# A planned attention and feed-forward kernel: weight buffers cut from two areas, and four output tiles by seven block products with sums made by adding transfers

## The chip, the cores and the metric
The kernel runs on one core of a Trainium2 chip. A time is what one execution takes on the device, in microseconds (us); the metric is the median of several executions. Engines are called by their short names: PE multiplies matrices, DVE and ACT do element-wise work, POOL is the fifth engine, SP issues transfers.

## The reference
Attention with a soft cap (batch 2, 12 heads, 448 positions, head size 64), and behind it two feed-forward layers over 896 tokens, 768 wide inside and out and 2048 in the middle:

```
x   = attention(q, k, v)                      # 896 x 768
g1  = s * relu(x @ w1_in)**2 + b              # 896 x 2048
y   = g1 @ w1_out                             # 896 x 768
h   = y @ w2_in
out = (h * clip(h + 3, 0, 6) / 6) @ w2_out
```
All in float32. The weights arrive as raw 64-bit numbers and are turned into float32 on the core.

## The kernel before
**Products.** Each operand is split in two float32r parts, hi (the rounded value) and lo (the rest). One product of a 128x128 weight block with 128x448 columns is three matmuls into one PSUM bank: lo weight with hi value, hi with lo, hi with hi (`matmuls`, L232). Tokens come in two halves of 448 (`bi` 0 and 1).

**w_in by seven products.** `strassen` (L673) takes two weight tiles and both token halves as 2x2 blocks, and computes the four results by seven block products instead of eight (Strassen's scheme in Winograd's form). The sums of weight blocks S1 to S4 are made on DVE (L575 to L578), the sums of the right-hand blocks T1 to T4 once for a layer on DVE by `minus`. p1 and p2 make one result; p6 and p7 are added onto a copy of p1 in a bank `bb`, with the sums d1 and d2 between them on DVE.

**w_out plainly.** Each layer's w_out has six 128-row tiles (`mt`), and its 16 blocks of the middle dimension come in two halves of 8. For each tile and token half, 8 products are added into a bank. The sum of the first half waits in a slot as `partial` and is copied back into a bank by ACT before the second half (L771). At layer 1's end ACT scales the bank by 1/6 (L791), and SP stores it.

**Weights.** `convert` fetches a raw tile (three buffers), ACT rescales it (L215), DVE shifts and merges bits (L223, L229); for w_in ACT makes the low bits first (L219). `parts` then makes hi on ACT (L543) and lo on DVE (L545). All of this works in one tile `w` of eight blocks; hi and lo lie in groups `gA` (two) and `gB` (two). Activations, sums and stores use 84 slots of 448 columns.

**Order.** `Plan` sets the order of the whole feed-forward part before anything is issued. Each task has an engine, a cost and tasks that it comes after; due times run backwards from PE's list, and a greedy pass hands each engine the most urgent task whose inputs and buffers are free (PE may choose among 36). The engines then run their queues in exactly that order: an instruction that waits holds up all behind it on its engine. What comes before, attention (to 91 us), is written out by hand.

Of the kernel before, what the change touches and what calls it, by code (L numbers as in the profile page):

```python
# [26 lines left out]
HF = KF // 2  # L27
# [7 lines left out]
BYTES = (True, False)  # L35
SLOTS_A, SLOTS_B = 36, 48
GROUPS = {"gA": 2, "gB": 2}
# [3 lines left out]
class Res:  # L41


    def __init__(self, kind, tile=None):
        self.kind, self.tile, self.left, self.held, self.order = kind, tile, 0, tile is not None, None


class Task:
    def __init__(self, engine, cost, run, after, use, number):
        self.engine, self.cost, self.run, self.use, self.number = engine, cost, run, use, number  # L50
        self.after = list(dict.fromkeys(t for t in after if t is not None))
        self.then, self.due, self.start, self.end = [], 1e9, None, None


class Plan:
# [5 lines left out]
    def __init__(self, sizes):  # L61
        self.tasks, self.sizes, self.pe = [], sizes, []
# [11 lines left out]
    def order(self):  # L74
# [3 lines left out]
        for t in reversed(self.tasks):  # L78
            for s in t.then:
                t.due = min(t.due, s.due - t.cost - self.LAG)  # L80
        for t in self.tasks:
            if t.soon is not None:
                t.due = min(t.due, max([a.due + a.cost for a in t.after if a.engine == "PE"], default=0.0) + t.soon)
        for t in reversed(self.tasks):
            if t.engine != "PE":
                for s in t.then:
                    t.due = min(t.due, s.due - t.cost - self.LAG)
        free = dict(self.sizes)
        banks, seen = 0, {}
# [12 lines left out]
        waiting = {e: [] for e in ("PE", "DVE", "ACT", "DMA")}  # L102
# [3 lines left out]
        for e in ("DVE", "ACT", "DMA"):  # L106
# [4 lines left out]

        def kind_of(u):
            kinds = u.kind if isinstance(u.kind, tuple) else (u.kind,)
            return next((k for k in kinds if free.get(k, 0) > 0), None)

        while left:
            moved = True
            while moved:
                moved = False
                for e, queue in waiting.items():  # L120
                    if idle[e] > now + 1e-9:
                        continue
                    for t in queue[:self.WINDOW] if e == "PE" else queue:
                        if any(a.end is None or a.end + (0 if a.engine == e else self.LAG) > now + 1e-9 for a in t.after):
# [4 lines left out]
                        for u in want:  # L129
                            k = kind_of(u)  # L130
                            if k is None or (u.kind == "bank" and u.order != next_bank):
                                ok = False
                                break
                            need[u] = k
                            free[k] -= 1
                        if not ok:
                            for k in need.values():
                                free[k] += 1
                            continue
                        for u, k in need.items():  # L140
                            u.held, u.kind = True, k
                            if k == "bank":
                                next_bank += 1
                        t.start, t.end = now, now + t.cost
                        idle[e] = t.end
# [5 lines left out]
            times = [x for x in idle.values() if x > now + 1e-9]  # L151
            times += [t.end + self.LAG for t in done[-80:] + ends if t.end + self.LAG > now + 1e-9]
# [4 lines left out]
            for t in [t for t in ends if t.end <= now + 1e-9]:  # L157
                ends.remove(t)
                done.append(t)
                for u in t.use:  # L160
                    u.left -= 1
                    if u.left == 0:
# [12 lines left out]
def attention_moe_moe(ctx: ExitStack, tc: tile.TileContext, qk, v, cap, w1i, w1o, s, b, w2i, w2o, out):  # L175
    nc = tc.nc
    const = ctx.enter_context(tc.tile_pool(name="const", bufs=1))
    sa = ctx.enter_context(tc.tile_pool(name="sa", bufs=SLOTS_A))
# [9 lines left out]
    whole = const.tile([128, 8, BL], F32, name="w")  # L188
    zeros = sa.tile([128, S], F32, name="zeros", tag="s")
    slot = lambda name, dt=F32R: sa.tile([128, S], dt, name=name, tag="s")  # L190
    x = [[[slot(f"x{p}{bi}{k}") for p in ("h", "l")] for k in range(KD)] for bi in range(B)]
    flat = whole.rearrange("p n m -> p (n m)")

    pools_w = {"gA": wp}
# [3 lines left out]

    def group(kind):
        n = 4 * BL if kind == "gA" else 3 * BL  # L200
        return [pools_w[kind].tile([128, n], F32R, name=f"{kind}{p}", tag=f"{kind}{p}", bufs=GROUPS[kind]) for p in ("h", "l")]
# [7 lines left out]
    def rescale(raw, n, bits, dve=False):  # L209
        up = raw_up(raw, n).bitcast(F32)  # L210
        up = up.rearrange("p (n m) -> p n m", m=BL) if len(bits.shape) == 3 else up
# [13 lines left out]
    def merge(raw, n, bits, mask=0x80000007, low=False):  # L225
        part = raw[:, :n, 0 if low else 1]
        part = part.rearrange("p (n m) -> p n m", m=BL) if len(bits.shape) == 3 else part
# [155 lines left out]
    def take(p):  # L383

        xu[p] = slot("xf", F32)
        nc.vector.tensor_copy(xu[p], pav.pop(p)[:, :S])

    def scale_x(p, engine=nc.vector.tensor_copy):
        bi, hp = divmod(p, H // 2)
        last = p >= P - 2  # L390
        if last:
            xu[p] = slot("xf", F32)
# [11 lines left out]
    first_groups, raws = {}, {}  # L404
# [4 lines left out]
    def early_region(i):  # L409

        if i < FIRST:
            return flat[:, i * CI:(i + 1) * CI]
        at = {FIRST: 1, FIRST + 1: 0, FIRST + 2: 4}[i]
        return whole[:, at:min(at + 4, 8):2, :] if at % 4 == 0 else whole[:, at:at + 3:2, :]
# [11 lines left out]
    def early_upper(i, dve=False):  # L426
        if i % 2 == 0:
            first_groups[i // 2] = group("gA")
        hi = first_groups[i // 2][0][:, i % 2 * CI:(i % 2 + 1) * CI]
        (nc.vector.tensor_copy if dve else nc.scalar.copy)(hi, early_region(i))  # L430

    def early_lower(i):
        hi, lo = (t[:, i % 2 * CI:(i % 2 + 1) * CI] for t in first_groups[i // 2])
        nc.vector.tensor_sub(lo, early_region(i), hi.bitcast(F32))

    def early_w(i, k):
        sl = slice(i % 2 * CI + k * 128, i % 2 * CI + (k + 1) * 128)
        return [t[:, sl] for t in first_groups[i // 2]]
# [11 lines left out]
    def feed_forward(sb):  # L450
# [529 lines left out]
```

## Time and profile before

| | us |
|---|---|
| three executions | 544.96, 540.43, 544.74 |
| their median | 544.74 |
| profiled execution, its own time | 539.42 |
| its span, first to last instruction | 537.6 |
| PE busy in the span | 529.6 |

The profile is of one execution. A matmul's shown length (366 ns for 448 columns) overlaps the next one's, so the distance from one start to the next is what a matmul costs PE. DVE and ACT instructions overlap a little too. In a chain of waits a row gives where a piece starts, how long it lasts and what it is.

### The profile page before, as it was taken

How to read it: one execution, taken by the hardware profiler on the slowest of the kernel's cores; microseconds unless marked ns; L12 is line 12 of the kernel's file. 1: busy time of each engine (PE TensorE's matmuls, PEld its weight loads, DVE VectorE, ACT ScalarE, POOL GpSimd, SP SyncE). 2: the span in 40 equal slices, each digit the busy share in tenths (PEclk: the TensorE clock that was granted, in tenths of full speed). 3: DMA queues.
4: the chain of work that ended last, by engine and by line, in shares of the span. 5: the costliest groups of instructions: out<-in, count | busy, mean ns of one | idle time of the engine just before them, and what ended most of it. 6: DMA issues, size and time to landing. Idle time of an engine off the chain costs nothing.

```text
span 537.6 us, 7211 instructions
## 1 busy us (share of the span) xinstructions
PE 529.6 (99%) x2768; PEld 437.4 (81%) x2768; DVE 412.6 (77%) x627; ACT 382.2 (71%) x521; POOL 0.6 (0%) x8
## 2 busy tenths in 40 slices
PE   8999999999999999999999999999999999999997
PEld 3232335998999999989999999999999999999996
DVE  2789999999997647889887888898756378997300
ACT  6999998696965657998567777964467479866201
POOL 0000000000000000000000000000000000000000
PEclk9999999999999999999999999999999999999999
DMA  8835412313036523224354233234544132236211
GB/s 316 334 111 185 129 36 87 122 36 95 30 97 214 176 81 117 99 79 133 102 177 152 89 112 99 78 95 113 176 173 144 66 98 79 79 116 187 77 51 51
DMA packets 17796, 64.36 MB, mean 120 GB/s; under 512 B 2402, under 2 KB 5730, under 8 KB 17634
## 3 DMA queue, kind: packets, MB, share of 16 engines
q1 hardware_dynamic: 17616, 63.75, 35.9%
q8 instruction: 21, 0.34, 0.3%
q10 hardware_dynamic: 146, 0.16, 0.1%
q14 instruction: 13, 0.11, 0.1%
HBM read 61.11 MB, written 2.79 MB: 119 GB/s over the span
## 4 chain that ended last, share of the span: by engine, by line
PE 92%; ACT 5%; DVE 2%; issue 1%; DVEq 0%; ACTq 0%
PE pf L234 39%; PE pav L234 30%; PE pz L234 10%; PE ps L267 5%; PE pav L293 4%; ACT t L275 2%; PE pav L290 1%; PE pz L330 1%; PE ps L271 1%; ACT raw L219 1%; ACT t L280 1%; PE pz L858 1%; ACT w L215 0%; DVE sl L488 0%; DVE gAl L545 0%
## 5 line engine op out<-in xcount | busy, mean ns | idle before, releaser
L229 DVE SCALAR_TENSOR_TENSOR w<-raw,w 128x512 uint32<-128x512 uint32 (+1 forms) x131 | 96.2, 758 | 21.8 <-ACT raw L219 20.5
L234 PE MATMUL pf<-sl,gBh 128*128 128x448 f32 x316 | 90.0, 366 | 0.0
L234 PE MATMUL pf<-sl,gAh 128*128 128x448 f32 x288 | 81.9, 366 | 0.0
L215 ACT ACTIVATE w<-raw 128x512 f32<-128x512 f32 (+1 forms) x79 | 58.4, 762 | 23.0 <-DMA raw<-in_w2o 9.0
L234 PE MATMUL pav<-sl,gAh 128*128 128x448 f32 x252 | 71.8, 366 | 0.0
L234 PE MATMUL pav<-sl,gBh 128*128 128x448 f32 x234 | 66.6, 366 | 0.0
L234 PEld LDWEIGHTS pf<-sl,gBh 128*128 128x128 f32 x316 | 59.4, 188 | 5.1
L234 PE MATMUL pf<-sl,gBl 128*128 128x448 f32 x158 | 57.9, 366 | 0.0
L234 PEld LDWEIGHTS pf<-sl,gAh 128*128 128x128 f32 x288 | 54.1, 188 | 4.4
L219 ACT ACTIVATE raw<-raw 128x768 uint16<-128x768 uint16 x29 | 55.7, 1966 | 0.1
L234 PE MATMUL pf<-sl,gAl 128*128 128x448 f32 x144 | 52.7, 366 | 0.0
L543 ACT CAST gBh<-w 128x1152 fp32r<-128x1152 f32 (+1 forms) x27 | 29.8, 1104 | 31.6 <-DVE w L229 14.0
L234 PEld LDWEIGHTS pav<-sl,gAh 128*128 128x128 f32 x252 | 47.3, 188 | 4.0
L223 DVE TENSOR_SCALAR w<-w 128x512 uint32<-128x512 uint32 (+1 forms) x80 | 37.4, 475 | 17.0 <-ACT w L215 16.7
L545 DVE TENSOR_TENSOR gBl<-w,gBh 128x1152 fp32r<-128x1152 f32 (+1 forms) x27 | 34.8, 1289 | 18.9 <-ACT gBh L543 18.9
L234 PEld LDWEIGHTS pav<-sl,gBh 128*128 128x128 f32 x234 | 43.9, 188 | 3.6
L234 PE MATMUL pav<-sl,gAl 128*128 128x448 f32 x126 | 46.1, 366 | 0.0
L545 DVE TENSOR_TENSOR gAl<-w,gAh 128x1536 fp32r<-128x1536 f32 (+2 forms) x26 | 38.9, 1496 | 9.4 <-ACT gAh L543 9.3
L543 ACT CAST gAh<-w 128x1536 fp32r<-128x1536 f32 (+2 forms) x26 | 33.1, 1274 | 16.6 <-DVE w L229 13.2
L234 PE MATMUL pav<-sl,gBl 128*128 128x448 f32 x117 | 42.8, 365 | 0.0
L280 ACT ACTIVATE t<-t 128x896 f32<-128x896 f32 x42 | 39.9, 950 | 1.2
L275 ACT ACTIVATE t<-ps 128x896 f32<-128x896 f32 x42 | 37.9, 902 | 3.3 <-PE ps L267 3.3
(161 smaller groups left out, 901.4 us busy)
## 6 DMA issues: line engine op xcount, KB each, us to landing
raw<-in_w1i SPq DMA_DIRECT2D x16, 768.0 KB, 5.5
raw<-in_w1o SPq DMA_DIRECT2D x24, 512.0 KB, 3.7
raw<-in_w2i SPq DMA_DIRECT2D x16, 768.0 KB, 4.9
raw<-in_w2o SPq DMA_DIRECT2D x24, 512.0 KB, 4.2
rqk<-in_qk SPq DMA_DIRECT2D x11, 448.0 KB, 4.4
out<-sl SPq DMA_DIRECT2D x12, 224.0 KB, 1.9
rb<-rows SPq DMA_DIRECT2D x10, 224.0 KB, 3.6
va<-in_v SPq DMA_DIRECT2D x1, 1344.0 KB, 14.0
```

The source lines that it names most:

```text
L215: nc.scalar.activation(bits, up, AF.Copy, scale=2.0**-112)
L219: nc.scalar.activation(by[:, :, 2], by[:, :, 1], AF.Copy, scale=2.0**-13, bias=0.5**14 - 0.5)
L223: nc.vector.tensor_scalar(bits, bits, 3, None, op0=ALU.logical_shift_left)
L229: nc.vector.scalar_tensor_tensor(out=bits, in0=part, scalar=29 if low else mask, in1=bits, op0=ALU.logical_shift_right if low else ALU.bit ...
L234: nc.tensor.matmul(ps[:, :S], w[a], rhs[r], start=start and i == 0, stop=stop and i == 2, skip_group_check=True)
L267: nc.tensor.matmul(ps[:, j, :S], raw_qk[p][rows, 1, c * 128:(c + 1) * 128], raw_qk[p][rows, 0, :], start=True, stop=True)
L271: nc.tensor.matmul(ps[keys, col, :S], raw_qk[p + o][rows, 1, NC * 128:], raw_qk[p + o][rows, 0, :], start=True, stop=True)
L275: nc.scalar.activation(u_t[n], u_ps.pop(n)[:, :, :S], AF.Tanh, scale=icap_r)
L280: nc.scalar.activation(u_t[n], u_t[n], AF.Exp, scale=cap_r)
L293: nc.tensor.matmul(pav[p][(top, end)[j], :S], va[bi][:, d, (2 * (p % 2) + j) * NC + c, :], u_t[n][:, j, :], start=(p % 2 == 0 and c == 0), ...
L543: nc.scalar.copy(part(0), cols)
L545: c = add("DVE", dve(n), lambda: nc.vector.tensor_sub(part(1), cols, part(0).bitcast(F32)), [a], [g])
```

## The change
Buffers of the feed-forward part are no longer slots and groups: two areas of SBUF are handed out in columns by the plan itself (`Space`), 448-column tiles from one end and weight tiles from the other. A weight tile's lo part is now written over the converted weight itself (`low_of`). So a tile of converted weights is held per pair, not one for all, and the plan can convert several pairs ahead. The sums S1 to S4 are made inside the pair's own tiles.

At layer 1's end the last four w_out tiles (`OUT_ORDER[2:]`) of the second half go by seven products, two tiles at a time: 28 products of three matmuls a pair instead of 32. For this the sums of g are needed, for each of four block pairs `j`: four chained sums over 448-column tiles. They are made by 16 transfers that add onto their destination, issued by POOL (`accumulate`), after ACT has negated two operands; ACT and DVE then split each sum into hi and lo (`split_sum`). `partial` is no longer copied into a bank for these tiles but added when the result leaves it, mostly on DVE. `LOWS` says for which of a pair's four raw tiles ACT makes the low bits. The planner also counts an arrival time behind transfers (`late`) and lets ACT start at most 30 us ahead of a due time (`AHEAD`).

```diff
-BYTES = (True, False)
-SLOTS_A, SLOTS_B = 36, 48
-GROUPS = {"gA": 2, "gB": 2}
+LOAD = 0.004, 3.0
+AHEAD = {"ACT": 30.0}
+SUM_ISSUE, SUM_LATE = 1.2, 6.0
+SEVENS = 2
+LOWS = (True, False, True, False)
+SPACE = 36 * S + 12 * CI, 48 * S + 6 * CI
...
+    def take(self, n):
+        for area in ((1, 0) if n == S else (0, 1)):
+            for a, b in self.free[area] if n == S else reversed(self.free[area]):
+                if b - a >= n:
+                    at = a if n == S else b - n
+                    self.cut(area, at, n)
+                    return area, at
+        return None
...
+        def parts(f, after, before=()):
+
+            h = res(f.n)
+            a = add("ACT", acts(f.n), lambda: nc.scalar.copy(t_of(h, F32R), f.tile), after, [f, h])
+            c = add("DVE", dve(f.n), lambda: nc.vector.tensor_sub(low_of(f), f.tile, h.tile.bitcast(F32)), [a, *before], [f, h])
+            return (h, f), [a, c]
...
+        def out_pair(layer, mts, half):
+
+            f1, f2, f3 = res(3 * CO), res(2 * CO), res(2 * CO)
...
+            s1 = sums(f1, 2, f2, 1, f3, 0, CO, nc.vector.tensor_add, [m21, m22])
+            s2 = sums(f2, 0, f1, 2, f1, 0, CO, nc.vector.tensor_sub, [m11, s1])
+            s3 = sums(f2, 1, f1, 0, f2, 1, CO, nc.vector.tensor_sub, [m11, s1])
+            s4 = sums(f3, 1, f1, 1, f2, 0, CO, nc.vector.tensor_sub, [m12, s2])
+            (g1, t1), (g2, t2), (g3, t3) = parts(f1, [m12, s1], [s2, s3, s4]), parts(f2, [s2, s3], [s4]), parts(f3, [s4])
...
+        def accumulate(r, other, after):
+
+            t = add("POOL", SUM_ISSUE, lambda: nc.gpsimd.dma_start(out=r.tile, in_=other.tile, accum_op=ALU.add), after, [r, other])
+            t.late = SUM_LATE
+            return t
...
+        def sums_of_g(half):
+
+            n = HF // 2
+            ops = {x: [] for x in ("T1", "T2", "T3", "T4")}
+            for j in range(n):
+                f = half * HF + j
+                (b11, e11), (b12, e12), (b21, e21), (b22, e22) = [GF[f + k, bi] for k in (0, n) for bi in range(B)]
+                n12, f12 = negative(b12, e12)
+                n21, f21 = negative(b21, e21)
+                d3 = accumulate(b22, n12, [f12, e22, *G[f + n, 1].tasks])
+                d1 = accumulate(n12, b11, [d3, e11])
+                d2 = accumulate(b11, b22, [d1, d3, *G[f, 0].tasks])
+                d4 = accumulate(n21, b11, [d2, f21])
+                for x, t, d, sign in (("T3", b22, d3, 1), ("T1", n12, d1, -1), ("T2", b11, d2, 1), ("T4", n21, d4, -1)):
+                    ops[x].append(split_sum(t, d, sign))
...
+                if m == 0:
+                    pe[mark:mark] = first
+                    pe.extend(fifth + sixth + second)
+                else:
+                    pe.extend(first + tail[:len(tail) // 3] + fifth + tail[len(tail) // 3:] + sixth + second)
+                tail = seventh + last
+            pe.extend(tail)
```

**How the order changes, place 1: DVE at the start of the feed-forward part.** PE's 181st matmul there needs the lo part of the second pair's first weight tile, a subtraction over 1536 columns. Names w, gAl are the old weight tiles and groups, sl slots; m and two numbers name a piece of the new areas. Before:

```order
L638 SCALAR_TENSOR_TENSOR sl_916<-sl_916,st_66 128x448
L229 SCALAR_TENSOR_TENSOR w_71<-raw_933,w_71 128x2x384
L576 TENSOR_TENSOR w_71<-w_71 128x384
L488 TENSOR_TENSOR sl_1118<-sl_1043,sl_1103 128x448
L488 TENSOR_TENSOR sl_1125<-sl_1049,sl_1105 128x448
L488 TENSOR_TENSOR sl_1134<-sl_1055,sl_1113 128x448
L577 TENSOR_TENSOR w_71<-w_71 128x384
L578 TENSOR_TENSOR w_71<-w_71 128x384
L488 TENSOR_TENSOR sl_1149<-sl_1065,sl_1120 128x448
L488 TENSOR_TENSOR sl_1154<-sl_1074,sl_1127 128x448
L545 TENSOR_TENSOR gAl_1143<-w_71,gAh_1142 128x1536
```

And now:

```order
L755 TENSOR_TENSOR m75_1042<-m35_106,m32_103 128x448
L290 SCALAR_TENSOR_TENSOR m70_1015<-raw_943,m70_1015 128x768
L599 TENSOR_TENSOR m70_1015<-m70_1015 128x384
L599 TENSOR_TENSOR m62_978<-m70_1015,m62_978 128x384
L599 TENSOR_TENSOR m62_978<-m70_1015 128x384
L553 TENSOR_TENSOR m81_1075<-m65_995,m74_1040 128x448
L553 TENSOR_TENSOR m82_1080<-m67_1002,m77_1053 128x448
L589 TENSOR_TENSOR m84_1087<-m70_1015,m80_1069 128x1536
L553 TENSOR_TENSOR m87_1103<-m73_1038,m78_1058 128x448
```

Counted from the first sum of x's blocks (98.96 us in the trace of before), 41 DVE instructions stood ahead of that subtraction, and 28 do now; most of the sums of x moved behind it.

**Place 2: PE and POOL at layer 1's end.** Before, PE ran 8 products of one tile and one token half after another; the last bank begins

```order
L234 MATMUL pav_912<-sl_3876,gBl_4397 128x448
L234 MATMUL pav_912<-sl_3893,gBh_4396 128x448
L234 MATMUL pav_912<-sl_3876,gBh_4396 128x448
L234 MATMUL pav_912<-sl_3853,gBl_4397 128x448
L234 MATMUL pav_912<-sl_3865,gBh_4396 128x448
L234 MATMUL pav_912<-sl_3853,gBh_4396 128x448
```

Now PE comes to the first operand that hangs on the last pair's g (T1 of j = 3, written m567_4487 and m569_4495), to T2 of j = 0 and to T1 of j = 2:

```order
L295 MATMUL pf_895<-m567_4487,m527_4275 128x448
L295 MATMUL pf_895<-m569_4495,m524_4251 128x448
L295 MATMUL pf_895<-m567_4487,m524_4251 128x448
L295 MATMUL pav_917<-m560_4456,m533_4306 128x448
L295 MATMUL pav_917<-m564_4470,m526_4273 128x448
L295 MATMUL pav_917<-m560_4456,m526_4273 128x448
L295 MATMUL pf_895<-m571_4505,m527_4275 128x448
L295 MATMUL pf_895<-m573_4515,m524_4251 128x448
L295 MATMUL pf_895<-m571_4505,m524_4251 128x448
```

Between the end of p7 of the last w_in pair (bank pf_915, whence g of block 15 comes) and the second of these rows stand 124 matmuls; up to the lo part of T2 of j = 3 stand 157, and of T4 of j = 3 211. POOL, which issued no transfer before, issues 16, of which these are the last 12 (destination first; j = 3 and j = 2 alternate with j = 1 and 0):

```order
L764 DMA m525_4267<-m491_4045 128x448
L764 DMA m529_4285<-m498_4078 128x448
L764 DMA m472_3941<-m509_4150 128x448
L764 DMA m458_3825<-m514_4184 128x448
L764 DMA m491_4045<-m496_4071 128x448
L764 DMA m498_4078<-m469_3917 128x448
L764 DMA m530_4291<-m472_3941 128x448
L764 DMA m528_4280<-m458_3825 128x448
L764 DMA m496_4071<-m525_4267 128x448
L764 DMA m469_3917<-m529_4285 128x448
L764 DMA m547_4386<-m496_4071 128x448
L764 DMA m544_4370<-m469_3917 128x448
```

m525_4267 takes d3 of j = 3, m491_4045 then d1, m496_4071 d2, m547_4386 d4: each waits until the one before it has landed.

**Place 3: DVE at layer 1's end.** Before, the last DVE rows were the conversion of the last two tiles:

```order
L545 TENSOR_TENSOR gAl_4342<-w_71,gAh_4341 128x1024
L223 TENSOR_SCALAR w_71<-w_71 128x512
L229 SCALAR_TENSOR_TENSOR w_71<-raw_4283,w_71 128x512
L223 TENSOR_SCALAR w_71<-w_71 128x512
L229 SCALAR_TENSOR_TENSOR w_71<-raw_4331,w_71 128x512
L229 SCALAR_TENSOR_TENSOR w_71<-raw_4283,w_71 128x512
L229 SCALAR_TENSOR_TENSOR w_71<-raw_4331,w_71 128x512
L545 TENSOR_TENSOR gBl_4397<-w_71,gBh_4396 128x1024
```

Now, from the sum d2 of the last w_in pair (it waits for p7) to the lo part of g's block 15, behind which POOL may issue d3 of j = 3:

```order
L728 TENSOR_TENSOR m523_4249<-pf_915,m506_4127 128x448
L599 TENSOR_TENSOR m507_4132<-m516_4195 128x512
L599 TENSOR_TENSOR m507_4132<-m516_4195,m507_4132 128x512
L599 TENSOR_TENSOR m504_4104<-m516_4195,m507_4132 128x512
L589 TENSOR_TENSOR m527_4275<-m516_4195,m524_4251 128x1536
L677 SCALAR_TENSOR_TENSOR m525_4267<-m525_4267,m523_4249 128x448
L677 SCALAR_TENSOR_TENSOR m529_4285<-m529_4285,pf_895 128x448
L285 TENSOR_SCALAR m522_4233<-m522_4233 128x512
L589 TENSOR_TENSOR m533_4306<-m507_4132,m526_4273 128x1024
L691 TENSOR_TENSOR m536_4318<-m525_4267,m531_4298 128x448
```

and some 25 rows further the lo parts that PE's rows above need (L773), behind weights of the second pair:

```order
L589 TENSOR_TENSOR m565_4476<-m537_4320,m558_4444 128x1536
L773 SCALAR_TENSOR_TENSOR m569_4495<-m491_4045,m567_4487 128x448
L589 TENSOR_TENSOR m570_4503<-m532_4304,m553_4417 128x1024
L773 SCALAR_TENSOR_TENSOR m573_4515<-m498_4078,m571_4505 128x448
```

Of the 37 DVE instructions from that d2 to the lo part of T1 of j = 3, 16 are over 448 columns, 13 over 512, two over 1536, two over 1024, and four are shifts over 512; before, nothing after the last block of g stood on DVE but conversions.

## Rows read from the trace of the kernel before

**Rows 1.** Page, part 1: busy time, share of the span, instructions.
```profile
PE 529.6 (99%) x2768; PEld 437.4 (81%) x2768; DVE 412.6 (77%) x627; ACT 382.2 (71%) x521; POOL 0.6 (0%) x8
```

**Rows 2.** Waits of PE: total us, times, longest us.
```profile
PE ps L267 <- ACT t L275: 1.0, 2, 0.7
PE pf L234 <- DVE gAl L545: 0.3, 1, 0.3
```

**Rows 3.** Chain of waits, feed-forward part: start us, us, what.
```profile
103.91 10.95 PE pav L234 x54
...
130.09 7.44 PE pf L234 x36
...
174.73 14.88 PE pav L234 x72
...
234.57 3.65 PE pf L234 x18
...
390.51 9.72 PE pf L234 x48
```

**Rows 4.** Timeline of PE at two starts: start us, us, what, idle before.
```profile
125.24 0.57 PE L234 MATMUL pf<-sl,gAh 128*128 128x448 f32 x2
126.11 0.47 PE L234 MATMUL pf<-xh,gAl 128*128 128x448 f32 x1 [0.30 <-DVE gAl L545]
...
229.96 0.57 PE L234 MATMUL pf<-sl,gBh 128*128 128x448 f32 x2
230.66 0.47 PE L234 MATMUL pz<-xh,gAl 128*128 128x448 f32 x1
```

**Rows 5.** Stretches: busy us of each engine, granted clock, DMA share.
```profile
460.00:480.00 20.00, 20.00 (x101) 18.53 (x100) 19.90 (x35) 14.48 (x27) 0.00 (x0) 1.00 0.34 107
480.00:500.00 20.00, 20.00 (x100) 18.54 (x99) 15.96 (x26) 12.36 (x21) 0.00 (x0) 1.00 0.56 177
500.00:520.00 20.00, 20.00 (x100) 18.53 (x99) 2.15 (x3) 3.77 (x6) 0.00 (x0) 1.00 0.13 47
520.00:540.00 20.00, 14.02 (x70) 12.64 (x68) 0.00 (x0) 1.64 (x4) 0.00 (x0) 0.93 0.12 46
```

**Rows 6.** Timeline of DVE, runs without a gap and the start.
```profile
98.96 1.69 DVE L717 TENSOR_TENSOR sl<-xf 128x448 f32<-128x448 f32 x3
...
124.30 1.75 DVE L545 TENSOR_TENSOR gAl<-w,gAh 128x1536 fp32r<-128x1536 f32 x1
...
471.67 2.75 DVE L654 TENSOR_TENSOR sl<-sl 128x448 fp32r<-128x448 f32 x5
...
492.29 1.90 DVE L229 SCALAR_TENSOR_TENSOR w<-raw,w 128x512 uint32<-128x512 uint32 x3
```

**Rows 7.** Groups by line and form, DVE: mean ns of one.
```profile
L654 DVE TENSOR_TENSOR sl<-sl 128x448 fp32r<-128x448 f32 x40 | 24.1, 619 | 2.5 <-ACT sl L648 2.1
L545 DVE TENSOR_TENSOR gAl<-w,gAh 128x1536 fp32r<-128x1536 f32 x14 | 24.5, 1753 | 2.6 <-ACT gAh L543 2.5
L545 DVE TENSOR_TENSOR gBl<-w,gBh 128x1024 fp32r<-128x1024 f32 x13 | 15.9, 1220 | 4.5 <-ACT gBh L543 4.5
L223 DVE TENSOR_SCALAR w<-w 128x512 uint32<-128x512 uint32 x48 | 19.8, 421 | 7.5 <-ACT w L215 7.4
```

**Rows 8.** Timeline of ACT: a run of casts, and the last instruction.
```profile
101.47 2.44 ACT L485 CAST sl<-sl 128x448 fp32r<-128x448 f32 x5
...
534.06 0.54 ACT L791 ACTIVATE sl<-pav 128x448 f32<-128x448 f32 x1 [4.33 <-PE pav L234]
```

**Rows 9.** DMA issues: KB each, median us to landing.
```profile
raw<-in_w2i SPq DMA_DIRECT2D x16, 768.0 KB, 4.9
out<-sl SPq DMA_DIRECT2D x12, 224.0 KB, 1.9
rb<-rows SPq DMA_DIRECT2D x10, 224.0 KB, 3.6
va<-in_v SPq DMA_DIRECT2D x1, 1344.0 KB, 14.0
```

More of the change, by code (lines that the diff above doesn't have):

```diff
@@ L51, in __init__ @@
         self.after = list(dict.fromkeys(t for t in after if t is not None))
-        self.then, self.due, self.start, self.end = [], 1e9, None, None
+        self.then, self.due, self.start, self.end, self.late = [], 1e9, None, None, 0.0
 class Plan:
@@ L79, in order @@
             for s in t.then:
[L80 removed]
+                t.due = min(t.due, s.due - t.cost - t.late - self.LAG)
+        made = {}
         for t in self.tasks:
+            made[t] = max([a.due + a.cost if a.engine == "PE" else made[a] for a in t.after], default=0.0)
             if t.soon is not None:
[L83 removed]
+                t.due = min(t.due, made[t] + t.soon)
         for t in reversed(self.tasks):
@@ L86, in order @@
                 for s in t.then:
-                    t.due = min(t.due, s.due - t.cost - self.LAG)
+                    t.due = min(t.due, s.due - t.cost - t.late - self.LAG)
         free = dict(self.sizes)
+        space = Space(SPACE, {(*u.at, u.n) for t in self.tasks for u in t.use if u.kind == "mem" and u.held} | set(self.taken))
         banks, seen = 0, {}
@@ L101, in order @@
                     free[u.kind] = free.get(u.kind, 0)
-        waiting = {e: [] for e in ("PE", "DVE", "ACT", "DMA")}
+        waiting = {e: [] for e in ("PE", "DVE", "ACT", "DMA", "POOL")}
         for t in self.tasks:
@@ L105, in order @@
         waiting["PE"] = list(self.pe)
-        for e in ("DVE", "ACT", "DMA"):
+        for e in ("DVE", "ACT", "DMA", "POOL"):
             waiting[e].sort(key=lambda t: (t.due, t.number))
@@ L123, in order @@
                     for t in queue[:self.WINDOW] if e == "PE" else queue:
-                        if any(a.end is None or a.end + (0 if a.engine == e else self.LAG) > now + 1e-9 for a in t.after):
+                        if e in AHEAD and now < t.due - AHEAD[e]:
+                            continue
+                        if any(a.end is None or a.end + (0 if a.engine == e and e != "POOL" else self.LAG) > now + 1e-9 for a in t.after):
                             continue
@@ L151, in order @@
             times = [x for x in idle.values() if x > now + 1e-9]
+            times += [t.due - AHEAD[e] for e in AHEAD for t in waiting[e] if t.due - AHEAD[e] > now + 1e-9]
             times += [t.end + self.LAG for t in done[-80:] + ends if t.end + self.LAG > now + 1e-9]
@@ new lines, in convert @@
+            a = None
+            if raw is None:
+                a = add("DMA", n * LOAD[0], lambda: load_raw(tile_of(), src, n), (), [r])
+                a.late = LOAD[1]
+            if stage < 1:
+                a = add("ACT", acts(n, True), lambda: rescale(r.tile, n, bits()), [a], [r, f])
+            l = add("ACT", 0.0022 * n, lambda: low_bits(r.tile, n), [a], [r]) if low and stage < 2 else None
+            a = add("DVE", dve2(n), lambda: shift(bits()), [a], [f])
+            if low:
+                return add("DVE", dve(n), lambda: merge(r.tile, n, bits()), [a, l], [r, f])
@@ new lines, in convert @@
+            a = add("DVE", dve(n), lambda: merge(r.tile, n, bits(), 0x80000000), [a], [r, f])
+            return add("DVE", dve(n), lambda: merge(r.tile, n, bits(), low=True), [a], [r, f])
+        def parts(f, after, before=()):
[3 more added lines that the diff above has]
+            return (h, f), [a, c]
```

373 lines of the change are left out of this document (210 added, 163 removed).

## The prediction
> **What bounds the kernel now.** I began with the busy shares, and the reader is to see there that PE works 99% of the span [rows 1]. Then the waits of PE: from the feed-forward part on there is one that the page counts, 0.3 us [rows 2]. The chain of waits shows that from 130 us on PE alone sets the end, matmul behind matmul. So what counts is the number of matmuls, the distance from one start to the next, and any wait that the change adds.
>
> The distance is not one number. In the chain it is 10.95/54 = 202.8 ns before 126 us, 7.44/36 = 206.7 and 14.88/72 = 206.7 between 126 and 230 us, and 3.65/18 = 202.8 and 9.72/48 = 202.5 after that [rows 3]. The timeline shows PE beginning anew at 126.11 and at 230.66, each time after a small gap [rows 4], and the distance changes there and nowhere else. The granted clock is 1.00 in the stretches that I looked at [rows 5], so it is not the clock. I read it as a pace that PE falls into at each new start and keeps until the next one. About 2150 matmuls follow the last start before 91 us, so the two paces, 4.1 ns apart, are worth 2150 x 0.0041 = 8.8 us.
>
> **The change, part by part.**
>
> *Matmuls removed.* Four tiles by two token halves by 8 products were 64 products; two pairs by 28 are 56. 8 x 3 = 24 matmuls fewer, on the path: 24 x 0.2026 = 4.86 us.
>
> *Two new starts.* The matmul after 125.24 (two of them) was due at 125.24 + 2 x 0.203 = 125.65 and came at 126.11; the one after 229.96 was due at 230.37 and came at 230.66 [rows 4]. That is 0.46 + 0.29 = 0.75 us of gaps. The first waited for a subtraction on DVE that began at 124.30 [rows 6]. 13 DVE instructions fewer now stand ahead of it; at 0.53 us a step (below) it begins at 124.3 - 6.9 = 117.4, well ahead of 126. The second gap came where one pair was converted at a time; the new areas let several pairs be converted ahead. I take both gaps as gone (bounds: 0 and 0.75 us).
>
> *Work added to DVE and ACT.* DVE's step from one instruction to the next is shorter than its shown length: five over 448 columns take 2.75, one 0.619, so (2.75 - 0.619)/4 = 0.53 a step, 0.09 less than shown. Likewise (1.90 - 0.09)/3 = 0.60 over 512, 1.67 over 1536, 1.13 over 1024, and 0.34 for a shift [rows 6, 7]. ACT's step over 448 is about 2.44/5 = 0.49 [rows 8]. At layer 1's end DVE gets 16 lo parts, 8 weight sums, 6 sums between products, 6 outputs (28 over 448, 8 over 512: 14.9 + 4.8), longer lo parts (3.3), and loses four merges (2.4): some 21 us. ACT gets eight negations, 16 hi parts, four low bits, four copies between products and longer casts, and loses eight copies into banks and six outputs: some 15 us. From 480 us DVE is busy 15.96 and 2.15 of two stretches of 20, ACT 12.36 and 3.77 [rows 5], so the room is there and the work is beside PE. What matters is when each piece is ready.
>
> *DVE's queue at the place that matters.* Counted from the end of p7 of the last pair, T1 of j = 3 needs 37 DVE instructions: 16 x 0.53 + 13 x 0.60 + 2 x 1.67 + 2 x 1.13 + 4 x 0.34 = 23.3 us. PE comes to it after 124 matmuls, 25.1 us. Margin 1.8 us if DVE is not behind and never waits. DVE was at 19.90 of 20 us just before [rows 5], so a wait of 0 to 3 us is possible; I take 0.
>
> *The adding transfers.* d3 of j = 3 may be issued after the first ten of those DVE rows: 4 x 0.53 + 3 x 0.60 + 1.67 + 1.13 + 0.34 = 7.1 us. Call L the time from one transfer's release to the next one's. After the last one ACT and DVE need about 1.2 us for the hi and lo part. T1 hangs on two transfers, T2 (after 157 matmuls, 31.8 us) on three, T4 (after 211, 42.7 us) on four. PE does not wait as long as L is below (25.1 - 8.3)/2 = 8.4, (31.8 - 8.3)/3 = 7.8 and (42.7 - 8.3)/4 = 8.6 us.
>
> No row shows an adding transfer. The nearest below is a store of the same 224 KB, 1.9 us, or the same size from memory, 3.6; the adding one reads two such tiles and writes one, 672 KB in all, and a 768 KB load lands in 4.9; at the far end a 1344 KB load among many others took 14.0 [rows 9]. I take the 4.9 and 1.1 more for POOL's issue, which no row prices: L = 6. Ends: 1.9 and 14.0.
>
> DVE's shift over 512 columns shows 421 ns where its lo parts over 448, fewer columns, show 619 [rows 7], so it runs in a quicker mode. The Trainium skill (SBUF — State Buffer, section Who interferes with whom) says that DVE in such a two-port mode holds the port that POOL needs to write a transfer's descriptors, and that the transfer then waits for the instruction's end. No run here shows it, as POOL issued none. That rule speaks against this change: an estimate by it is up to 0.42 us more for each transfer, L = 6.4, still under 7.8.
>
> *The end.* The last matmul is still followed by one ACT output and one store; ACT began the last output at 534.06, 3.6 us before the span's end [rows 8]. Nothing changes there.
>
> **Rivals.**
>
> *The pace decides.* Without any new start before layer 1's end, PE keeps the pace of its start near 91 us. The sum with the quicker pace throughout: 539.42 - 4.86 - 0.75 - 500 x 0.0041 (the stretch from 126 to 230) = 531.8. With the slower one throughout: 531.8 + 8.8 = 540.6. For before, with its 24 matmuls and its gaps, the same two ends are 537.4 and 546.2, and its four executions (539.4, 540.4, 544.7, 545.0) lie 23, 34, 83 and 86% of the way up. This is no other mechanism of the change, but it is as large as its gain.
>
> *The transfers are slow.* With L above 7.8 PE waits three or four times the excess. At L = 9.6 the wait is 3 x 1.8 = 5.4 us, and the gain is gone. At L = 12 T4 comes 4 x 12 + 8.3 - 42.7 = 13.6 us late: 537 + 13.6 = 550.6, slower than before by 1%. For it: the chain of four has no neighbour in the trace, POOL's queue is in order, and weight loads share the engines. Against: the loads of three times the tile land in 4.9. The rule on the shared port makes it a little likelier. Chance 0.1.
>
> *The queues stand in each other's way.* ACT and DVE now wait for transfers in the middle of their queues, with casts of the second pair's weights behind. A first transfer that comes some 5 us late, or DVE a little behind at p7, would cost PE 2 to 5 us: 540 to 543. For it: DVE's margin of 1.8 us; against: PE never waited in the DVE-full stretch before 480. Chance 0.17.
>
> *It doesn't do what it says.* The 24 matmuls are gone from PE's list, so this could only be by waits, as above.
>
> **How the numbers follow.** The likeliest case (0.73) has no new wait of size. Against its own time the profiled execution gives 539.42 - 4.86 - 0.75 = 533.8 with its own mix of paces. That execution is 5.3 us under the median of 544.74. The four executions of before lie on the mean 57% of the way up, and 531.8 + 0.57 x 8.8 = 536.8; I forecast 537. Range 531 to 543: both paces, and the queue case; the slow transfers (0.1) and the far part of the rest stay out.
>
> A measurement of this kernel can tell about 1% from no change: its own three executions span 0.8%. The gain without the paces, 5.6 us, is 1.0%, so faster and same are close. Faster by over 1% means under 539.3: 0.62 of the likeliest case, 0.45, and a little of the queue case, 0.47 in all. Same 0.45. Slower by over 1% (above 550.2) only by slow transfers, 0.08.
>
> **What would show it.** In the profile after: 24 PE matmuls fewer; PE's waits in the feed-forward part none or under 1 us; no gap at 126 or 230; 16 transfers on a queue that had none, with 5 to 7 us from issue to landing and POOL free in between. A wait of PE on DVE or ACT for T1, T2 or T4 of j = 3 (lines 772 to 776) over 2 us makes the forecast wrong; the releaser behind it, a transfer or an instruction of DVE's queue, tells the second rival from the third. The distance of matmul starts tells the first: 202.6 throughout would give 532, 206.7 throughout 541.

## The result and the profile after

| us | before | the change |
|---|---|---|
| median of 21 executions each | 541.78 | 535.38 |
| lowest and highest | 537.79, 546.12 | 534.26, 541.42 |
| profiled execution, its own time | 539.42 | 534.26 |
| its span | 537.6 | 532.5 |

The ratio is 0.9888, 95% interval 0.9863 to 0.9913: shorter by 1.1%, 1.6 us under the forecast. The gain is clear of zero, but the interval, 0.9 to 1.4%, doesn't settle whether it is over the 1% that the prediction set for faster. The ratios here and below leave out executions over 1.5% above a kernel's fastest (six of before's, at 717 to 2975 us, and seven of experiment 1 at PE's slow pace), so the clusters of runs stand beside them.

The table hides the most telling thing. Before's runs are spread over 8 us; 20 of the change's 21 lie between 534.3 and 536.2, and one at 541.4.

The page's first part after, to be held against [rows 1]:

```profile
PE 523.0 (98%) x2744; PEld 433.3 (81%) x2744; DVE 436.4 (82%) x661; ACT 397.8 (75%) x541; POOL 14.8 (3%) x24
```

The 24 matmuls are gone. DVE has 23.8 us more, ACT 15.6. But PE is busy 98%, not 99%: it waits more than before. Its waits behind 91 us (total us, times, longest us), which answer to [rows 2]:

```profile
PE pav L295 <- DVE pav L724: 1.4, 1, 1.4
PE pf L295 <- DVE pf L724: 0.2, 1, 0.2
```

and the timeline of PE at the places (start us, us, what, idle before), which answers to [rows 4]:

```profile
127.44 1.99 PE L295 MATMUL pav<-m,m 128*128 128x448 f32 x9
129.65 7.84 PE L295 MATMUL pf<-m,m 128*128 128x448 f32 x36 [0.23 <-DVE pf L724]
137.33 3.82 PE L295 MATMUL pav<-m,m 128*128 128x448 f32 x18
142.58 3.71 PE L295 MATMUL pav<-m,m 128*128 128x448 f32 x17 [1.44 <-DVE pav L724]
...
164.58 11.10 PE L295 MATMUL pf<-m,m 128*128 128x448 f32 x54
175.52 14.76 PE L295 MATMUL pav<-m,m 128*128 128x448 f32 x72
190.12 5.03 PE L295 MATMUL pf<-m,m 128*128 128x448 f32 x24
...
498.98 1.12 PE L295 MATMUL pf<-m,m 128*128 128x448 f32 x3
499.93 0.77 PE L295 MATMUL pav<-m,m 128*128 128x448 f32 x3
```

A row's idle is counted from a matmul's shown end, so I count from starts, at 0.2027 us a matmul. From 127.44 to 137.33, 45 matmuls took 9.89 us where 9.12 were due: 0.77 lost, in two pauses. The start at 142.58 was due at 137.33 + 18 x 0.2027 = 140.98: 1.60 late, and the matmul behind a start costs 0.1 more. From 498.98 on 0.95 us passed for 0.61: 0.34 lost. The change loses 2.8 us in pauses. Before lost 0.57 and 0.40 us counted in the same way at the two starts of [rows 4], and 0.29 at a third that I had not seen, here in its timeline (347.50 was due):

```profile
347.09 0.57 PE L234 MATMUL pf<-sl,gAh 128*128 128x448 f32 x2
347.69 0.47 PE L234 MATMUL pf<-sl,gAl 128*128 128x448 f32 x1
```

The pace after is the quick one: (190.12 - 175.52)/72 = 202.8 ns where before had 206.7 [rows 3]; it is quick from 91 us to the end. The rows of granted clock that stand ahead of the prediction are of quick stretches alone [rows 5]; in before's slow stretch it was 1.00 too, with the same columns:

```profile
140.00:160.00 20.00, 20.00 (x99) 18.16 (x98) 18.32 (x33) 15.38 (x26) 0.00 (x0) 1.00 0.17 54
```

So the two profiled executions differ by -24 x 0.2027 = -4.86, +1.57 of pauses, and -502 x 0.0040 = -2.0 for before's slow stretch from 126 to 230 us: -5.3, measured -5.16. For the medians, where before's runs hold more of the slow pace, -6.40 = -4.86 + 1.57 - 3.1; the last term is what the other two leave, and I put it down to the pace. **The pace gave as much as the pauses took, and more.**

DVE after, at the places of [rows 6]:

```profile
116.84 1.75 DVE L589 TENSOR_TENSOR m<-m,m 128x1536 fp32r<-128x1536 f32 x1
...
137.54 2.47 DVE L675 SCALAR_TENSOR_TENSOR m<-m,st 128x448 f32<-128x448 f32 x4
139.92 1.47 DVE L689 SCALAR_TENSOR_TENSOR m<-m,bt,m 128x448 fp32r<-128x448 f32 x2
141.31 0.68 DVE L675 SCALAR_TENSOR_TENSOR m<-m,st 128x448 f32<-128x448 f32 x1
141.91 0.62 DVE L724 TENSOR_TENSOR pav<-pav,m 128x448 f32<-128x448 f32 x1
...
473.35 0.62 DVE L728 TENSOR_TENSOR m<-pf,m 128x448 f32<-128x448 f32 x1
...
497.08 0.61 DVE L773 SCALAR_TENSOR_TENSOR m<-m,m 128x448 fp32r<-128x448 f32 x1
...
498.75 0.61 DVE L773 SCALAR_TENSOR_TENSOR m<-m,m 128x448 fp32r<-128x448 f32 x1
```

The subtraction over 1536 columns began at 116.84 (forecast 117.4), and the wait at 126 went. The sum d1 at 141.91 is the next thing late: PE's p7 needs it, and it stands behind seven element-wise steps of the first blocks of g. The stretches of the end (PE, PEld, DVE, ACT, POOL, granted clock, DMA share, GB/s), against [rows 5]:

```profile
480.00:500.00 20.00, 19.92 (x99) 18.15 (x98) 19.72 (x32) 17.31 (x28) 10.59 (x12) 1.00 0.91 182
500.00:520.00 20.00, 20.00 (x101) 18.54 (x99) 8.28 (x14) 4.60 (x9) 0.00 (x0) 1.00 0.26 75
```

DVE is full to 500 us. The transfers on POOL's timeline, and their row of the DMA issues, against [rows 9]:

```profile
481.07 2.66 POOL L764 DMA_DIRECT2D m<-m  x3 [6.25 <-DVE m L691]
...
486.65 0.87 POOL L764 DMA_DIRECT2D m<-m  x1 [1.05 <-issue]
...
492.79 0.87 POOL L764 DMA_DIRECT2D m<-m  x1 [0.27 <-issue]
...
497.43 0.86 POOL L764 DMA_DIRECT2D m<-m  x1 [2.44 <-ACT pav L815]
...
m<-m POOLq DMA_DIRECT2D x16, 224.0 KB, 4.4
```

d3, d1, d2 and d4 of j = 3 were issued at 481.07, 486.65, 492.79 and 497.43: L was 5.6, 6.1 and 4.6 us.

### The profile page after: what moved, and what is told of

Same layout as the page of the kernel before. It is cut to its first block, busy times and chain, and to the rows that moved or that the text cites. A ratio compares the mean times of both kernels' runs of the same rounds, so it can differ in the third digit from the quotient of the medians.

```text
span 532.5 us, 7301 instructions
## 1 busy us (share of the span) xinstructions
PE 523.0 (98%) x2744; PEld 433.3 (81%) x2744; DVE 436.4 (82%) x661; ACT 397.8 (75%) x541; POOL 14.8 (3%) x24
## 5 line engine op out<-in xcount | busy, mean ns | idle before, releaser
L295 PE MATMUL pf<-m,m 128*128 128x448 f32 x1068 | 226.4, 366 | 0.3 <-DVE pf L724 0.2
L295 PEld LDWEIGHTS pf<-m,m 128*128 128x128 f32 x1068 | 200.4, 188 | 17.9 <-issue 0.9
L295 PE MATMUL pav<-m,m 128*128 128x448 f32 x837 | 178.7, 366 | 1.4 <-DVE pav L724 1.4
L295 PEld LDWEIGHTS pav<-m,m 128*128 128x128 f32 x837 | 157.2, 188 | 14.1 <-DVE pav L724 1.8
L290 DVE SCALAR_TENSOR_TENSOR m<-raw,m 128x512 uint32<-128x512 uint32 (+1 forms) x127 | 94.4, 761 | 16.5 <-ACT raw L281 14.4
L589 DVE TENSOR_TENSOR m<-m,m 128x1024 fp32r<-128x1024 f32 (+2 forms) x54 | 76.0, 1413 | 19.8 <-ACT m L588 19.1
L588 ACT CAST m<-m 128x1024 fp32r<-128x1024 f32 (+2 forms) x54 | 65.1, 1208 | 28.4 <-DVE m L290 21.8
L277 ACT ACTIVATE m<-raw 128x512 f32<-128x512 f32 (+1 forms) x79 | 60.0, 767 | 11.4 <-PE pav L295 4.3
L281 ACT ACTIVATE raw<-raw 128x768 uint16<-128x768 uint16 (+1 forms) x33 | 62.1, 1890 | 0.5
L295 PE MATMUL pz<-m,m 128*128 128x448 f32 x249 | 53.9, 365 | 0.0
```

Of the source, the lines that this page charges most:

```text
L277: nc.scalar.activation(bits, up, AF.Copy, scale=2.0**-112)
L281: nc.scalar.activation(by[:, :, 2], by[:, :, 1], AF.Copy, scale=2.0**-13, bias=0.5**14 - 0.5)
L290: nc.vector.scalar_tensor_tensor(out=bits, in0=part, scalar=29 if low else mask, in1=bits, op0=ALU.logical_shift_right if low else ALU.bit ...
L295: nc.tensor.matmul(ps[:, :S], w[a], rhs[r], start=start and i == 0, stop=stop and i == 2, skip_group_check=True)
L588: a = add("ACT", acts(f.n), lambda: nc.scalar.copy(t_of(h, F32R), f.tile), after, [f, h])
L589: c = add("DVE", dve(f.n), lambda: nc.vector.tensor_sub(low_of(f), f.tile, h.tile.bitcast(F32)), [a, *before], [f, h])
```

## Experiments

The open questions: what made the new pauses, whether the transfers matter, and what sets the pace, by which a run gains or loses up to 8 us.

**1. The buffers without the seven products**, twice.

```diff
-SEVENS = 2
+SEVENS = 6
...
-            else:
+            elif sevens:
                 out_sevens(layer, sevens, partial, mark)
```

> The new buffers and their order stay, but all six w_out tiles of layer 1's second half go by plain products: 24 matmuls more than the change, no sums of g, no transfers by POOL. Theory of the sum: 24 x 0.2027 = 4.86 us more than the change, less the 0.35 us that the change waits at 499 us; 535.4 + 4.5 = 539.9 us in the median, with a spread as narrow as the change's (20 of 21 runs within 2 us), since the new starts of PE at 129 to 143 us are the buffers' and stay. Rival: the narrow spread came with the seven products; then the runs scatter as before's do, from 538.8 to 547.5, median about 543.

539.55 us (538.74 to 547.53), ratio to before 0.9965 (0.9918 to 1.0012). Seven of 12 runs lie at 538.7 to 539.6, five at 546.6 to 547.5. A second time:

> The new buffers and their order without the seven products, a second time, on the same chip as the next one. If its start at 143 us is drawn slow in 5 of 12 for good: 2 to 4 of 6 runs at 546.5 to 547.5, the others at 538.7 to 539.6. If the chip or the hour made it: all or none.

539.68 us; eight of 12 at 539.0 to 540.1, four at 546.4 to 547.5. So the median holds the sum (539.9 forecast), but the narrow spread didn't come with the buffers. The profile of the first is of one of the five: PE's timeline at the same start and after it

```profile
143.69 2.54 PE L295 MATMUL pav<-m,m 128*128 128x448 f32 x11 [1.44 <-DVE pav L724]
...
166.11 11.32 PE L295 MATMUL pf<-m,m 128*128 128x448 f32 x54
177.27 8.02 PE L295 MATMUL pav<-m,m 128*128 128x448 f32 x38
```

(177.27 - 166.11)/54 = 206.7 ns, and so to the end: 1925 matmuls x 4 ns = 7.7 us. The same pause of 1.6 us stands ahead of it as in the change. The profile of the second is quick throughout, 539.83 us; the change's second profile (experiment 5) is too, 535.43: 4.40 apart, where 4.86 - 0.45 of the pause at 500 us were due. In this plan the buffers alone gain nothing clear against before.

**2. The sums of g on DVE instead of adding transfers.**

```diff
-            t = add("POOL", SUM_ISSUE, lambda: nc.gpsimd.dma_start(out=r.tile, in_=other.tile, accum_op=ALU.add), after, [r, other])
-            t.late = SUM_LATE
-            return t
+            return add("DVE", dve(S), lambda: nc.vector.tensor_add(r.tile, r.tile, other.tile), after, [r, other])
```

> The 16 sums of g by DVE instructions instead of adding transfers (16 steps of 0.53 us, 8.5 us more on DVE, some 12 of them ahead of the lo part that PE waits for at 499 us). Theory A, DVE's queue is what the operands T1 of j = 3 and 2 wait for: PE waits 4 to 8 us more there, 539 to 543 us. Theory B, the chain of transfers is: without it the operands come earlier, the 0.35 us wait goes, 535 us.

535.06 us (534.42 to 535.24, 4 runs), as the change. Theory A falls in its size: DVE is full here too, but the plan put other work behind what PE waits for. DVE, granted clock, DMA share, GB/s:

```profile
474.00:500.00 26.00, 25.83 (x45) 1.00 0.27 94
500.00:520.00 20.00, 16.03 (x24) 1.00 0.14 51
```

The change has 8.28 us of DVE in the second stretch; the 8 us more went there, where PE needs little of it. Theory B falls too: the pause by T1 stayed (0.35 us at 505 us, where the change has 0.34). The adding transfers neither cost nor bring anything here.

**3. The planner's offsets**, two constants together: PE's start behind DVE's (`HEAD`), and the time from one engine to another (`LAG`).

```diff
-HEAD = 2.0
+HEAD = 0.5
...
-    LAG = 0.25
+    LAG = 0.35
```

> The change with two of the planner's constants nearer to the trace (PE's start 0.5 us behind DVE's instead of 2.0; 0.35 us from an instruction's end to its follower on another engine instead of 0.25). Theory of the late queue: the 1.7 us wait at 141 us and most of the smaller ones (0.50, 0.28, 0.35 us) come from DVE running 3 us later against PE than the plan has it, and go; the quick pace throughout would give 532 to 533 us. On the pace: if a long pause is what lets PE start quick, it is now drawn at short pauses and the runs scatter over 532 to 541 us; if the change's order starts quick anyway, the median is 533 with a narrow spread. Rival to the late queue: the wait at 141 us stays over 1 us, and the median at 535.

537.49 us (533.93 to 541.59), ratio 0.9933 (0.9885 to 0.9981). Its waits of PE:

```profile
PE pav L295 <- DVE pf L724: 0.6, 1, 0.6
PE pz L295 <- DVE m L589: 0.5, 1, 0.5
PE pav L295 <- DVE pav L724: 0.2, 1, 0.2
```

The wait at 141 us fell from 1.6 to 0.33 us by the starts, and those at 129, 131 and 499 went; two new ones came at 153 and 253 us, the first behind some shorter delays. So the pause was DVE's queue, planned too early. Yet the median rose: six runs lie at 533.9 to 535.1, six at 539.9 to 541.6. The last start is now at 253 us, 1361 matmuls before the end, 5.4 us between the paces. The profile is of a quick run (535.05); that the six others ran at the slow pace is read from their times. By that reading a better plan lost to the pace.

**4. Many starts.**

```diff
-    WINDOW = 36
+    WINDOW = 4
...
+                k = 0 if f == fs[-1] else (f // 2 + layer) % 3
...
-                    pe.extend(head + seventh + second + tail + last)
+                    pe.extend(head + seventh + second[:HK - k] + tail + last)
                 seventh, tail = next_seventh, next_tail
+                if f != fs[-1]:
+                    pe.extend(second[HK - k:] + seventh + tail)
+                    seventh, tail = [], []
```

> The change with the product p7 put right behind p6, or one or two products of p2 between, in ten pairs, and PE allowed to choose among 4 products rather than 36: PE then waits for d1 on DVE some 12 times, 0.4 to 2 us each, 10 to 16 us in all, 546 to 553 us. It is made for the pace behind each new start. Theory G: behind pauses of over 1 us PE is always quick (202.7 ns a matmul), behind shorter ones slow (206.7 ns) about half of the time. Theory D: a draw at each start whatever the pause, slow after a third to a half of them. Theory W: slow only behind waits for weights, so quick behind all of these, which are waits for a bank.

549.62 us (2 runs). PE pauses 12 times for 0.5 to 1.9 us. Behind three it is slow (128.26, 214.79, 455.18 us, pauses of 1.90, 0.88 and 1.72 us), behind nine quick (pauses of 0.49 to 1.67 us). At 214.79 it had been slow already. Between that pause and the next, two much shorter delays changed it too: behind one of 0.07 us at 224 us it was quick ((226.69 - 224.86)/9 = 203.3 ns), behind one of 0.11 us at 228 us slow again. Two of the pauses in PE's timeline:

```profile
455.18 2.12 PE L295 MATMUL pf<-m,m 128*128 128x448 f32 x9 [1.56 <-DVE pav L724]
457.14 2.02 PE L295 MATMUL pav<-m,m 128*128 128x448 f32 x9
459.00 3.88 PE L295 MATMUL pf<-m,m 128*128 128x448 f32 x18
...
469.91 2.09 PE L295 MATMUL pf<-m,m 128*128 128x448 f32 x9 [1.45 <-DVE pz L724]
471.84 1.99 PE L295 MATMUL pz<-m,m 128*128 128x448 f32 x9
473.67 3.81 PE L295 MATMUL pf<-m,m 128*128 128x448 f32 x18
```

(459.00 - 457.14)/9 = 206.7 ns against (473.67 - 471.84)/9 = 203.3. Neither a long pause (theory G) nor the kind of wait (theory W) decides. A quarter slow is fewer than theory D has (a third to a half), but of the three it alone is left.

**5. Whose chance it is.** The change again, unedited:

> The change itself, a second time, beside the variants. In its first 21 runs PE started slow at 143 us once; the kernel with its buffers alone, whose PE waits are the same up to 430 us, did in 5 of 12. Theory D, each start is a draw of about the same chance: 4 to 6 of 12 runs at about 541.5 here too, the others at 534.3 to 536. Theory P, the chance belongs to the program: at most one of 12.

535.52 us (534.51 to 535.93, 6 runs): with the first 21, quick in 26 of 27, by their times and the two profiles. Then with one matmul more at the very start:

```diff
-WARM = (S, S, S // 4)
+WARM = (S, S, S // 4, 16)
```

> The change with one more small matmul (16 columns) among those that warm PE up before the first inputs arrive, which moves nothing else but the place of every later PE instruction in its program. The change started quick at 143 us in 26 of 27 runs. If that chance hangs on such a detail of the program: some of 6 runs at 541.5. If it is set by what PE waits for there: at most one, the others at 534.3 to 536.

535.9 us, seven of 12 runs at 534.7 to 535.9 and five at 541.3 to 542.4. One in 27 against five in 12 is hardly chance (exact test, p = 0.007). So the change's narrow spread seems a property of this very program, and with one matmul of 16 columns ahead of all inputs it is gone. The two didn't run on the same chip; on the chip of the second, before's slow runs were no more frequent than in its first 44 (11 of 32 at 543.6 us and above, against 21), which speaks against the chip but doesn't rule it out. The profile here is of a quick run. What in the program does it stays open.

**6. A plan without pauses.** DVE planned 4% longer, the constants of experiment 3, and the squares of three more blocks (0, 1 and 3; the expectation names two) moved to ACT:

```diff
-SQUARES = (5, 7, 9, 11)
-HEAD = 2.0
+SQUARES = (0, 1, 3, 5, 7, 9, 11)
+HEAD = 0.5
...
-    LAG = 0.25
+    LAG = 0.35
...
-        dve = lambda n, scalar=False: 0.075 + 0.00104 * n + (0.06 if scalar else 0)
+        dve = lambda n, scalar=False: 1.04 * (0.075 + 0.00104 * n) + (0.06 if scalar else 0)
```

> The change with the plan made stricter (PE 0.5 us behind DVE, 0.35 us from engine to engine, DVE steps 4% longer) and two more of layer 0's squares on ACT for the first blocks (0 and 1), so that DVE has less to do at 130 to 150 us. Theory of the late queue: no wait of PE behind 92 us of over 0.3 us. PE then keeps the pace of the start at 92 us, quick in all six profiles so far: 532.0 to 533 us with a narrow spread, the best of all kernels. Rival D: the start at 92 us is a draw as well, or small pauses remain and each is one: runs up to 541, median between 533 and 538.

532.60 us (531.56 to 538.72), ratio 0.9843 (0.9781 to 0.9906); beside the change's 535.52 on the same chip. PE has no wait at all behind 92 us, and the page's chain of waits is almost all PE's:

```profile
PE 96%; ACT 3%; issue 1%; DVE 0%
```

Its profiled execution took 532.59, the change's 535.43: 2.84 less, the change's pauses (2.89 us in that profile). A second time:

> The stricter plan with the seven products and the adding transfers a second time, for its spread. In the plain variant of it PE fell from the quick pace to the slow one at 316 us with no pause at all, where one weight load began 14 ns late behind a copy on ACT. So a start is not needed, any late release can do it. If that is rare: at most 3 of 12 runs over 534, median 532.6 us, ratio to before near 0.983. If it is as common as behind pauses: a third or more of the runs at 535 to 541, median up to 535.

532.48 us, ratio 0.9891 (0.9832 to 0.9951). Of the 12 runs nine lie at 531.6 to 532.6, three at 537.8 to 538.9, as many as the expectation allowed. **Nine of 12 beat every run of both kernels**, and it isn't safe from the slow pace. With the sums of g on DVE as well (blocks 1 and 3's squares on ACT, 0.3 us from engine to engine):

> The same stricter plan (0.5 us, 0.3 us, 4%; block 1 and 3's squares on ACT too), with the sums of g by DVE instructions instead of adding transfers. The plan has room for the 16 instructions behind 500 us, as it had without the stricter constants (535.06 us against the change's 535.38). If the transfers are worth nothing, it comes out as the stricter plan with transfers does, within 1 us, 532 to 533; if they relieve DVE now that PE waits nowhere else, PE waits 1 to 4 us at 497 to 510 us, 534 to 537.

532.47 us, ratio 0.9858 (0.9797 to 0.9918); four of six runs at 532.3 to 532.5, two at 536.8 and 537.7. As far as two plans that also differ in one block's squares and in 0.05 us can tell, the transfers are worth nothing here either.

**7. The same plan without the seven products, and with the old buffers.** The edits of 6 on the kernel of 1, and on the kernel before.

> The stricter plan that left PE without a pause, with all w_out tiles by plain products (24 matmuls more, no sums of g). If the seven products are worth their matmuls and nothing else, it is 24 x 0.2027 = 4.9 us above the same plan with them: 532.6 + 4.9 = 537.5 us, PE without a wait. Rival: the sums, transfers and splits of the seven products cost something that is hidden in no trace row; then the difference is under 4 us.

537.27 us, ratio 0.9949 (0.9908 to 0.999). The fastest run is 536.41 against 531.56 with the seven products: 4.85 us, where the 24 matmuls are 4.86; between the medians of the lower clusters it is 4.6 (536.94 and 532.35, on different chips). So nothing else of over 0.3 us is hidden. The profile of this kernel was of 541.42, with no wait of PE, and shows what I had ruled out. From its chain of waits:

```profile
303.12 4.86 PE pav L295 x24
307.98 10.37 PE pf L295 x51
...
325.80 3.72 PE pf L295 x18
```

4.86/24 = 202.5 ns ahead, 3.72/18 = 206.7 behind, and a mixed row between. The distances change at 316.13 us. There the timeline has, for a matmul shortly before and for that one, PE's matmul and the weight load that starts with it, and the copy on ACT that the next matmul's bank waits for:

```profile
315.57 0.53 ACT L715 COPY pav<-pf 128x448 f32<-128x448 f32 x1
315.72 0.37 PE L295 MATMUL pf<-m,m 128*128 128x448 f32 x1
315.72 0.19 PEld L295 LDWEIGHTS pf<-m,m 128*128 128x128 f32 x1
316.13 0.37 PE L295 MATMUL pf<-m,m 128*128 128x448 f32 x1
316.15 0.19 PEld L295 LDWEIGHTS pf<-m,m 128*128 128x128 f32 x1
```

The load starts with its matmul in the first pair (2 to 4 ns behind it as a rule), 16 ns behind in the second: it waited for the copy, which ended at 316.10. No view of waits counts 14 ns. From there to the end the pace is the slow one, 1063 matmuls x 4.0 ns = 4.3 us. That the late load is the cause is not shown, and it is not enough by itself: in the second profile of experiment 6 the same load came 24 ns behind its matmul, behind the same copy, and the distance stayed (3.65/18 = 202.8 ns):

```profile
316.25 0.36 PE L295 MATMUL pf<-m,m 128*128 128x448 f32 x1
316.28 0.19 PEld L295 LDWEIGHTS pf<-m,m 128*128 128x128 f32 x1
...
325.74 3.65 PE pf L295 x18
```

Eleven other loads in the kept profiles came 13 to 105 ns behind their matmul in a quick stretch, and the pace stayed quick behind each.

> The kernel before with the same stricter constants. With one tile of converted weights for all pairs the plan itself has PE wait 0.8, 0.1 and 2.2 us where weights of the next pairs are late. If the new buffers are what lets a plan without pauses exist: pauses of 2 to 3 us in all on PE, and runs scattered from 539 to 548 us. If the stricter constants alone do it, without the new buffers: no pause, 537.5 us.

539.98 us, ratio 1.0002 (0.9966 to 1.0038). Of its three waits of PE behind 92 us, 2.1 us in all, the longest:

```profile
PE pf L234 <- DVE gAl L545: 1.5, 1, 1.5
...
```

Late weights, as the plan itself had them; by the starts PE lost 2.9 us. Seven of the 12 runs of each kernel form the lower cluster, at 536.4 to 537.3 with the new buffers and 539.1 to 540.0 with the old: what the new buffers bring, with the planner's other changes (`LOWS`, `AHEAD`, `late`), is a plan without these pauses, once its constants are right.

## Why the prediction was right, and where not

The forecast of 537 lies 1.6 us above the median, by two errors of opposite sign: the pauses cost 2.8 us that it had at nothing, and 5.0 us of slow pace that it had counted (57% of 8.8) hardly came. That they nearly cancel is luck.

*24 matmuls, 4.86 us:* right; 4.85 between the fastest runs of experiments 6 and 7, 4.6 between their lower clusters.

*Two gaps taken as gone (bounds 0 and 0.75):* **this step failed.** Both went, and so did the third, at 347 us, that I had not seen. The first went for the reason given; with the old buffers in experiment 7 PE still paused at 229, 237 and 348 us (0.5, 0.7 and 1.8 us), which fits the reason for the second. But four others of 2.8 us in all came, outside the bounds. I followed the queue to the wait that the trace of before showed, and asked for no later one. The planner's offset was in the code: it has PE start 2 us behind DVE, where the trace of after has 1.1 (DVE's first planned instruction at 98.97 us, PE's at 100.08). And DVE loses some 0.2 us at instructions that find their input just arriving: the two at 139.92 took 1.47 us, where by the four before them, (2.47 - 0.68)/3 = 0.60 a step, 1.28 were due. By the plan's own times DVE was 3 us late against PE at 141 us. Experiment 3 shows it: with the two constants nearer to the trace most of the wait goes.

*The pace, 57% of the way up:* the two levels and their worth were right (202.7 and 206.7 ns; the all-quick floor of 531.8, which counted no pause, is what experiment 6 reached, 531.6 to 532.6). That it changes only at a new start was wrong: once it changed with no pause at all (experiment 7). And a mean over before's runs doesn't carry over: the change was quick in 26 of 27 runs, as it seems by a detail of its program (experiment 5). That is worth some 3.1 us of the 6.4.

*DVE's queue:* 23.3 us from the end of p7 to the end of T1's lo part of j = 3 were forecast. From the start of d2 it was 497.69 - 473.35 = 24.3, and d2 began 0.35 us behind p7's last matmul, whose shown end is 473.00. PE came to the lo part at 497.97, so that of the margin of 1.8 us some 0.3 were left. T1 of j = 2, 1.67 us behind it, made PE wait 0.34. The queue case was the one that happened, at a tenth of its size. The added work, over the whole span and in shown lengths, was 23.8 us on DVE (21 forecast) and 15.6 on ACT (15).

*The transfers:* L = 6 forecast, 4.6 to 6.1 measured, under 7.8. But they weren't what T1 hung on: d1 of j = 3 had landed (its successor was issued at 492.79) when DVE came to T1's lo part at 497.08. By the rule of the Trainium skill (SBUF — State Buffer, section Who interferes with whom) the estimate was up to 0.42 us more for a transfer beside a shift. In the profile after, a transfer's issue and a shift stand side by side:

```profile
484.60 1.00 POOL L764 DMA_DIRECT2D m<-m  x1 [0.87 <-issue]
...
485.09 0.42 DVE L285 TENSOR_SCALAR m<-m 128x512 uint32<-128x512 uint32 x1
```

The issue took 1.00 us, where those with no shift beside them and no other issue ahead take 0.86 to 0.89, and it ended 0.09 us behind the shift. In the kept profiles, the first issue of each aside, that is so of eleven issues, each with a shift that began 0.31 to 0.69 us behind the issue's start: they took 0.90 to 1.18 us and ended 0.07 to 0.09 us behind the shift. Where the shift was over within 0.66 us of the issue's start, as in 16 others, the issue took 0.86 to 0.88, and so it did in three where the shift began 0.67 us in. In the two profiles of experiment 5 one shift took 0.61 us itself beside two issues. So the trace bears the rule out for most shifts in the later part of an issue, with up to 0.3 us more. It changed nothing in the time: PE waited for no transfer, and experiment 2, which has none, took as long.

*The end:* the last output begins 3.8 us before the span's end, 3.6 forecast.

## What to carry to other kernels

A wait that a change removes uncovers the next in the same queue: follow the queue against the one that it feeds to its end, with the planner's offset between engines measured from the trace. Where an engine is busy 99%, look at the distance of its instructions as well as at its waits; two levels of it 2% apart can be worth more than the change. Two kernels are then compared by their clusters of runs, and a median that falls into one cluster by a detail of the program, as the change's seems to, is not a property that an edit keeps.

## What was not expected of the hardware

Each matmul here has its own weight load, and 448 columns take 202.7 or 206.7 ns from start to start at a granted clock of 1.00. The Trainium skill (TensorE: Matmul & The Clock Gate, section Wait — 56ns, not 53.3ns?) gives back-to-back matmuls as columns at 2.4 GHz and 2.5 ns more, by which an estimate is 189.2; no row here is that short, and the shortest single distance in the kept profiles is 196. PE mostly stays at either level for hundreds of matmuls. It changes level at some of its pauses, of 0.07 to 1.9 us, and stays at it through others; once it changed with no pause, at a weight load 16 ns behind its matmul, and 12 other loads 13 to 105 ns behind theirs changed nothing. How many runs hold the longer distance over much of their length differs by program. Read from their times, it is 1 run of 27 for the change, 5 of 12 with one more warm-up matmul, 9 of 24 with the buffers alone, 3 of 12 without pauses, and 21 of before's first 44 (543.6 to 546.1, with none between 541.8 and 543.6; of the 51 later ones that the ratios count seven lie between). Why remains open.
